# Whole 128x128 TensorE weights for the 64-query blocks of a sliding-window attention

## The chip, the cores and the metric

One core of a Trainium2 chip runs the whole program. The metric is the device time of one execution in microseconds (us), from the first to the last instruction with what the runtime puts around them. Times are medians of runs of the same program.

The engines are TensorE (PE; its weight loads are shown apart as PEld), VectorE (DVE), ScalarE (ACT), GpSimd (POOL) and SyncE (SP), which here issues all the transfers.

## The reference

Attention with a window of 128 keys and a linear bias for each head, then two MLPs. The inputs have batch 4, 8 heads, 576 positions and head dimension 64; there are 2304 tokens of width 512, and the hidden width is 2048.

```python
scores = scale * q @ k.T                         # for each batch and head, 576 x 576
rel = pos[:, None] - pos[None, :]
scores = where((rel >= 0) & (rel < 128), scores - slope[h] * abs(rel), -1e9)
attn = exp(scores - max); attn /= attn.sum(-1) + 1e-9
x = attn @ v                                     # to (2304, 512)
g = piecewise(x @ w_in1); x = g @ w_out1         # h | 0 | (h+1)^2/4
g = h2 * clip(h2 + 3, 0, 6) / 6; out = g @ w_out2    # h2 = x @ w_in2
```

## The kernel before

The queries are cut into twelve units (three for each batch of 576: 256+256+64, 192+256+128, 256+128+192, 192+256+128). A unit is computed for all eight heads, and for each head in blocks of 128 queries; a last block holds 64 queries where the unit's length is no multiple of 128. Those are unit 2 (a single block of 64), unit 3 (128 and 64), unit 8 (128 and 64) and unit 9 (128 and 64), so there are 4 x 8 = 32 blocks of 64. Units 0 to 3 are "whole": their attention is computed in plain float32, with unnormalized probabilities, and the row sum comes from a column of ones beside the values. Units 4 to 11 are "split": queries, keys, values and probabilities are split into a high and a low part of a faster format (fp32r), and the probabilities are normalized on GpSimd before they are transposed.

A step (head, block) passes through four stages, some ticks apart. `stage_a` (line 383 on) multiplies queries (the weights) with keys (moving) into PSUM on TensorE (line 380), VectorE adds the bias and finds the row's maximum (line 401), ScalarE takes the exponential (line 405), and for split units VectorE and GpSimd normalize (lines 408 to 410). Two ticks later `stage_b` transposes the probabilities on TensorE (lines 432 and 433), and ScalarE and VectorE copy and split them (lines 150 and 445). Then `stage_c_whole` (three ticks after stage a, line 463) or `stage_c` (four ticks, line 518) multiplies with the values; for whole units VectorE divides by the sums (lines 480 to 483), and `stage_d_whole` transposes the result (line 494). `prep` makes the high and low parts for a split head (lines 356 to 360, and 154/157 for the values of a pair of heads).

For a block of 64 queries the code before uses only the rows and columns that hold something: the scores' weights are 128 rows x 64 columns, the transposes have 64 rows, the value matmuls of whole units have weights of 128x64 (previous chunk of keys) and 64x64 (own chunk), and those of split units 64 rows x 128 columns for the own chunk.

Between the attention's ticks the first MLP runs in blocks of tokens: 24 matmuls per hidden chunk (12 at line 601 into `h`, 12 at line 643 into `acc`), with activations on VectorE, ScalarE and GpSimd. While the first three blocks run, its weights are also converted from float64 bits (lines 191 to 202). A hook spreads the attention's ticks over the MLP's chunks. On every engine but SP a planner orders the instructions by its own cost estimates and priorities; the order on SP is that of the program. All q, k and v transfers are on SP: for a pair of heads of a split unit keys and queries of the two heads (line 306, four transfers), then the values (lines 314 and 318). A transfer waits on SP until its buffer is free, and everything behind it on SP waits too. Keys and queries of split units have two buffers, values three.

Of the kernel before, what the change touches and what calls it, by code (L numbers as in the profile page):

```python
# [38 lines left out]
def tile_window_attention_two_mlps(  # L39
# [220 lines left out]
    class Attention:  # L260
# [19 lines left out]
        def load_whole(self, n):  # L280


            u = heads[n]
            q = self.qw[u.h // 2]
            for j in range(2):
                heads[n + j].k, heads[n + j].q = k, _ = self.kw[u.h + j], q
                nc.sync.dma_start(out=k[j * D:(j + 1) * D, :u.nk], in_=kT[u.b, u.h + j, :, u.k0:u.q1])
                if j == 0:
                    nc.sync.dma_start(out=q[:, :u.nq], in_=qT[u.b, u.h:u.h + 2, :, u.q0:u.q1].rearrange("h d n -> (h d) n"))

        def load(self, n):

            u = heads[n]
            if u.h % 2 == 0 and u.whole:
                self.load_whole(n)
            elif u.h % 2 == 0:
                self.k_owners.append(n)
                krs = self.raw.tile([P, 2, KMAX], F32, tag="kr", name=f"kr{n}")
                qrs = self.raw.tile([P, 2, UMAX], F32, tag="qr", name=f"qr{n}")
                for j in range(2):  # L300
                    heads[n + j].kr, heads[n + j].qr = krs[:, j], qrs[:, j]
                for j in range(2):
                    for dst, src, a, m in ((krs, kT, u.k0, u.nk), (qrs, qT, u.q0, u.nq)):
# [4 lines left out]
            if u.h % 2 == 0:  # L308
                self.v_owners.append(n)
                u.vt = self.vts[n // 2 % 3]  # L310
                u.vr = u.vt[:, :, 1:2 * D + 1]
                full, rest = divmod(u.nk, P)
                cols = slice(u.h * D, (u.h + 2) * D)
                nc.sync.dma_start(
                    out=u.vr[:, :full, :],
                    in_=v[u.b, u.k0:u.k0 + full * P, cols].rearrange("(c p) d -> p c d", p=P))
                if rest:
                    nc.sync.dma_start(out=u.vr[:rest, full, :],
                                      in_=v[u.b, u.k0 + full * P:u.k0 + u.nk, cols])
            else:  # L320
                u.vt, u.vr = heads[n - 1].vt, heads[n - 1].vr
# [23 lines left out]
        def prep(self, n):  # L345
# [14 lines left out]
            engines[LO["q"]].tensor_tensor(out=u.qs[:, :m], in0=u.qr[:, :m], in1=u.qs[:, :m].bitcast(F32), op=ALU.add)  # L360
            if u.h % 2 == 0:

                u.vs = self.proc.tile([P, 2, KCH, 2, D], F32R, tag="vs", name=f"vs{n}")
                full, rest = divmod(nk, P)
                parts = [(slice(0, P), slice(0, full))]
                if rest:
                    parts.append((slice(0, rest), slice(full, full + 1)))
                for pp, cc in parts:
                    for j in range(2):
                        src = u.vr[pp, cc, j * D:(j + 1) * D]  # L370
                        hi, lo = u.vs[pp, j, cc, j, :], u.vs[pp, j, cc, 1 - j, :]
                        split_hi(HI["v"], hi, src)
                        split_lo(LO["v"], lo, src, hi)
            else:
                u.vs = heads[n - 1].vs

        def scores(self, u, ps, qo, ko, m, nk):
            parts = [(u.q, u.k)] if u.whole else [(u.qs, u.kh), (u.qs, u.kl)]
            for w, (q, k) in enumerate(parts):
                nc.tensor.matmul(ps[:m, :nk], q[:, qo:qo + m], k[:, ko:ko + nk],  # L380
                                 start=(w == 0), stop=(w == len(parts) - 1))

        def stage_a(self, n, i):
# [11 lines left out]
            if u.unit == 0:  # L395
                keep_busy(ps, 2 * P)
            self.scores(u, ps, qo, ko, m, nk)
# [4 lines left out]
                out=pt[:m, :nk], in0=ps[:m, :nk], in1=dist[:m, u.h if u.whole else plain, bo:bo + nk],  # L402
                scale=-scale if u.whole else -slopes[u.h],
                scalar=3.0e38, op0=ALU.add, op1=ALU.min, accum_out=sm[:m, 0:1])
            nc.scalar.activation(out=pt[:m, :nk], in_=pt[:m, :nk], func=AF.Exp, bias=sm[:m, 0:1],  # L405
                                 scale=-1.0, accum_out=None if u.whole else sm[:m, 1:2])
            if not u.whole:
                nc.vector.tensor_scalar(out=sm[:m, 2:3], in0=sm[:m, 1:2], scalar1=EPS, scalar2=None, op0=ALU.add)  # L408
                nc.vector.reciprocal(sm[:m, 3:4], sm[:m, 2:3])  # L409
                nc.gpsimd.tensor_scalar(out=pt[:m, :nk], in0=pt[:m, :nk], scalar1=sm[:m, 3:4], scalar2=1.0,  # L410
                                        op0=ALU.mult, op1=ALU.mult)
            u.p[i] = pt

        def stage_b(self, n, i):
# [15 lines left out]
            po = P if has_prev else 0  # L430
# [3 lines left out]
            if has_prev and m == P:  # L434
                regs = [(slice(0, P), slice(0, 2), slice(s0, s0 + 2))]
            elif has_prev:
                regs = [(slice(0, P), slice(0, 1), slice(s0, s0 + 1)),
                        (slice(0, m), slice(1, 2), slice(s0 + 1, s0 + 2))]
            else:
                regs = [(slice(0, m), slice(1, 2), slice(s0 + 1, s0 + 2))]  # L440
            for pp, cs, cd in regs:
                src, hi = ps[pp, cs, :m], u.th[pp, cd, :m]
                split_hi(HI["th"], hi, src)
                if not u.whole:
                    nc.vector.tensor_tensor(out=u.tl[pp, cd, :m], in0=src, in1=hi.bitcast(F32), op=ALU.subtract)  # L445

        def stage_c_whole(self, n, i):
# [8 lines left out]
            rows = u.qbs[i][1]  # L456
            slot = 2 * i - 1 + sh
            work = [(i + sh, rows, slot + 1)]
            if slot >= 0:
                work.insert(0, (i - 1 + sh, P, slot))  # L460
            a = (2 * i + j) * (D + 1)
            for w, (c, keys, sl) in enumerate(work):
# [10 lines left out]
            nfull = u.nq // P  # L473
            parts = [(slice(0, P), slice(0, nfull))] if nfull else []
            if u.nq % P:
                parts.append((slice(0, u.nq % P), slice(nfull, nfull + 1)))
            for pp, bb in parts:
                nb = bb.stop - bb.start
                np_ = pp.stop
                nc.vector.tensor_scalar(out=rec[pp, bb], in0=r[pp, bb, 0:2 * D + 2:2 * D + 1], scalar1=EPS,  # L480
                                        scalar2=None, op0=ALU.add)
                nc.vector.reciprocal(rec[pp, bb], rec[pp, bb])
                nc.vector.tensor_tensor(
                    out=y[pp, bb], in0=r[pp, bb, 1:2 * D + 1].rearrange("p b (h d) -> p b h d", h=2),
                    in1=rec[pp, bb].rearrange("p b (h o) -> p b h o", o=1).to_broadcast([np_, nb, 2, D]), op=ALU.mult)
            u.y = y

        def stage_d_whole(self, n, i):
            u = heads[n]
            if u.h % 2 == 0 or i < len(u.qbs) - 1:  # L490
                return
            ps = psum.tile([P, BANK], F32, tag="t", name=f"x{n}")
            for b, (a, rows) in enumerate(u.qbs):
                nc.tensor.transpose(ps[:, b * P:b * P + rows], u.y[:rows, b].rearrange("p h d -> p (h d)"),
                                    ident[:rows, :rows])
            self.to_x(u, ps, LO["x_whole"])

        def stage_c(self, n, i):
# [11 lines left out]
            if i == 0 and u.prev:  # L510
                work.append((0, P, 0, u.qbs[0][1], 0))
            if i > 0:
                work.append((i - 1 + sh, P, (i - 1) * P, P + u.qbs[i][1], 2 * (i - 1) + sh))
            if last:
                work.append((i + sh, u.qbs[i][1], i * P, u.qbs[i][1], 2 * i + sh))
            for w, (c, rows, qo, nq, slot) in enumerate(work):
# [748 lines left out]
```

## Time and profile before

| what | value |
|---|---|
| median of 3 runs | 985.83 us (984.9 to 985.94) |
| the profiled execution's own time | 985.26 us |
| its span, first to last instruction | 983.5 us |
| mean granted TensorE clock | 0.998 of 2.4 GHz |
| busy: PE, PEld, DVE, ACT, POOL | 98%, 90%, 70%, 55%, 22% |
| attention's part of the span | about 4 to 515 us, beside the first MLP |

Matmuls are pipelined and their ends are modelled, so PE's busy share says little. How long TensorE takes for a matmul is read from the chain of waits, where consecutive pieces do not overlap, or from the starts of consecutive matmuls.

### The profile page before, as it was taken

The numbers are of one execution on the slowest core, as the hardware profiler recorded it, in microseconds if no ns is written. First come the engines' busy times: TensorE is split into PE (matmuls) and PEld (weight loads), VectorE is DVE, ScalarE is ACT, GpSimd is POOL, SyncE is SP. The second block draws the span as 40 slices with busy tenths as digits, with TensorE's granted clock in tenths as the row PEclk, the third lists the DMA queues.
The fourth block names the chain that finished last, engine by engine and source line by source line (L and its number), as shares of the span: only waits on it lengthen the run. The fifth ranks groups of instructions, "written<-read, shape, count | busy, mean of one in ns | idle before, by whom it ended". The sixth has DMA issues, their size and how long they took to land.

```text
span 983.5 us, 17188 instructions
## 1 busy us (share of the span) xinstructions
PE 959.4 (98%) x5771; PEld 885.4 (90%) x5771; DVE 685.6 (70%) x1768; ACT 544.3 (55%) x1334; POOL 220.7 (22%) x365
## 2 busy tenths in 40 slices
PE   8899999999999999999999999999999999999998
PEld 6787889999999998999999999999998888888987
DVE  6877886687777666767764898947747676644444
ACT  6886855577667566656653868534433334432323
POOL 2011234455455555545530000000000000000000
PEclk9999999999999999999999999999999999999999
DMA  9757313122213121222103875003354655353441
GB/s 261 218 160 240 107 52 110 51 81 82 71 43 86 50 73 42 70 70 68 52 1 118 271 274 183 1 0 118 139 182 150 207 179 161 122 156 117 117 117 68
DMA packets 95336, 114.90 MB, mean 117 GB/s; under 512 B 8848, under 2 KB 73616, under 8 KB 95248
## 3 DMA queue, kind: packets, MB, share of 16 engines
q1 hardware_dynamic: 95248, 113.80, 36.5%
q8 instruction: 46, 0.75, 0.3%
q14 instruction: 42, 0.34, 0.1%
HBM read 88.60 MB, written 25.17 MB: 116 GB/s over the span
## 4 chain that ended last, share of the span: by engine, by line
PE 80%; DVE 10%; ACT 4%; DMA 3%; issue 2%; SPq 0%; POOL 0%; ACTq 0%; DVEq 0%; POOLq 0%
PE h L601 24%; PE acc L702 17%; PE acc L643 17%; PE y L1166 5%; PE x L1166 4%; PE s L380 4%; PE r L518 3%; PE r L463 2%; PE t L432 2%; PE t L433 1%; DMA rawa<-w_out 1%; DVE kl L358 1%; DVE r L630 1%; DMA vr<-v 1%; DVE u L1175 1%
## 5 line engine op out<-in xcount | busy, mean ns | idle before, releaser
L601 PE MATMUL h<-x,wa 128*128 128x384 f32 (+1 forms) x1344 | 232.6, 318 | 4.4 <-DVE r L632 2.5
L643 PE MATMUL acc<-g,wa 128*128 128x384 f32 (+1 forms) x1344 | 229.2, 316 | 2.4 <-ACT o L150 1.2
L702 PE MATMUL acc<-wb,g 128*128 128x512 f32 x861 | 222.3, 394 | 0.0
L601 PEld LDWEIGHTS h<-x,wa 128*128 128x128 f32 x1344 | 207.6, 190 | 9.9 <-DVE r L632 3.7
L643 PEld LDWEIGHTS acc<-g,wa 128*128 128x128 f32 x1344 | 206.8, 190 | 5.7 <-ACT o L150 1.4
L702 PEld LDWEIGHTS acc<-wb,g 128*128 128x128 f32 x861 | 159.5, 188 | 24.9
L150 ACT CAST g<-r 128x384 fp32r<-128x384 f32 (+1 forms) x208 | 101.0, 487 | 81.1 <-DVE r L1113 42.6
L157 POOL TENSOR_TENSOR g<-r,g 128x256 fp32r<-128x256 f32 (+1 forms) x96 | 94.4, 985 | 196.6 <-ACT g L150 145.1
L631 ACT ACTIVATE r<-r 128x384 f32<-128x384 f32 (+1 forms) x112 | 53.3, 478 | 91.7 <-DVE r L630 90.4
L157 DVE TENSOR_TENSOR g<-r,g 128x384 fp32r<-128x384 f32 x112 | 62.3, 556 | 44.9 <-ACT g L150 44.4
L405 ACT ACTIVATE p<-p,sm 128x256 f32<-128x256 f32 (+2 forms) x160 | 75.9, 476 | 20.5 <-DVE sm L401 19.8
L630 DVE TENSOR_SCALAR r<-h 128x384 f32<-128x384 f32 (+1 forms) x112 | 55.3, 495 | 38.9 <-PE h L601 32.3
L632 DVE TENSOR_TENSOR r<-h,r 128x384 f32<-128x384 f32 (+1 forms) x112 | 55.4, 496 | 29.1 <-ACT r L631 28.5
L601 PE MATMUL h<-x,wb 128*128 128x384 f32 x384 | 72.5, 337 | 0.0
L601 PEld LDWEIGHTS h<-x,wb 128*128 128x128 f32 x384 | 68.2, 188 | 2.6
L401 DVE CUSTOM_DVE_ANT_0 p<-s,dist 128x256 f32<-128x256 f32 (+2 forms) x160 | 59.7, 374 | 14.9 <-PE s L380 13.3
L410 POOL TENSOR_SCALAR p<-p,sm 128x256 f32<-128x256 f32 (+1 forms) x104 | 47.8, 459 | 63.1 <-DVE sm L409 49.3
L360 POOL TENSOR_TENSOR qs<-qr,qs 128x256 fp32r<-128x256 f32 (+2 forms) x64 | 42.6, 665 | 26.9 <-ACT qs L357 24.4
L1112 ACT ACTIVATE r<-u 128x384 f32<-128x384 f32 x32 | 16.8, 525 | 55.6 <-DVE u L1175 55.6
L150 ACT CAST th<-t 128x256 fp32r<-128x256 f32 (+3 forms) x120 | 37.4, 312 | 14.7 <-PE t L433 12.8
L445 DVE TENSOR_TENSOR tl<-t,th 128x256 fp32r<-128x256 f32 (+3 forms) x120 | 41.6, 347 | 5.3 <-ACT th L150 4.0
L433 PE MATMUL t<-ident,p 128*128 128x128 f32 (+1 forms) x160 | 42.0, 264 | 2.7 <-DVE sm L408 2.1
(148 smaller groups left out, 1552.2 us busy)
## 6 DMA issues: line engine op xcount, KB each, us to landing
w<-wd SPq DMA_DIRECT2D x88, 256.0 KB, 2.7
rawa<-w_in SPq DMA_DIRECT2D x16, 512.0 KB, 5.5
rawa<-w_out SPq DMA_DIRECT2D x16, 512.0 KB, 5.5
rawb<-w_in SPq DMA_DIRECT2D x16, 512.0 KB, 4.2
rawb<-w_out SPq DMA_DIRECT2D x16, 512.0 KB, 5.5
wd<-sum SPq DMA_DIRECT2D x32, 256.0 KB, 2.1
wd<-wb SPq DMA_DIRECT2D x24, 256.0 KB, 2.9
out<-o SPq DMA_DIRECT2D x17, 256.0 KB, 2.2
```

The source lines that it names most:

```text
L150: nc.scalar.copy(hi, x)
L157: engines[eng].tensor_tensor(out=lo, in0=x, in1=hi.bitcast(F32), op=ALU.subtract)
L401: nc.vector.tensor_tensor_reduce(out=pt[:m, :nk], in0=ps[:m, :nk], in1=dist[:m, u.h if u.whole else plain, bo:bo + nk], scale=-scale if u. ...
L405: nc.scalar.activation(out=pt[:m, :nk], in_=pt[:m, :nk], func=AF.Exp, bias=sm[:m, 0:1], scale=-1.0, accum_out=None if u.whole else sm[:m, ...
L433: nc.tensor.transpose(ps[:m, 1, :m], pt[:m, po:po + m], ident[:m, :m])
L601: nc.tensor.matmul(ps[:, :n], self.W.w_in(a, c, f), self.x_chunk(x, b, c, n), start=(k == 0), stop=(k == 3 * KC - 1))
L630: nc.vector.tensor_scalar(out=r[:, :n], in0=ps[:, :n], scalar1=-1.0, scalar2=1.0, op0=ALU.max, op1=ALU.min)
L631: nc.scalar.activation(out=r[:, :n], in_=r[:, :n], func=AF.Square, bias=0.5, scale=0.5)
L632: nc.vector.tensor_tensor(out=r[:, :n], in0=ps[:, :n], in1=r[:, :n], op=ALU.max)
L643: nc.tensor.matmul(acc[i][:, o * n:(o + 1) * n], self.W.w_out(a, f)[:, e * P:(e + 1) * P], g[:, b, :n], start=(first and k == 0 and o == 0 ...
L702: nc.tensor.matmul(acc[t][:, :DM], g[:, b, tg * P:(tg + 1) * P], self.W.w_out(a, f), start=(first and k == 0), stop=(last and k == 2))
L1166: nc.tensor.matmul(ps[:, :N2], w[:, a, c * P:(c + 1) * P], self.x.operand(k, c, b), start=(start and n == 0), stop=(n == 5), skip_group_ch ...
```

## The change

Every block of 64 queries now uses weights of 128 rows and 128 columns. The scores read 128 query columns (64 of them zeros for split units, filled by a new GpSimd memset in `prep`, or whatever lies there for whole units). The bias, maximum and exponential run on 128 rows instead of 64. A new GpSimd memset sets the missing keys' probabilities (64 columns) to zero, the transposes are 128x128, and the value matmuls take all 128 keys. Where two instructions handled the full and the partial chunk apart (the copies of the transposes, the division by the sums, the values' high and low parts), one instruction remains.

Besides, for pairs of heads of split units the values' transfer is now issued ahead of the four transfers of keys and queries (`load_values`); for whole units it stays behind them.

```diff
         def load(self, n):
             u = heads[n]
             if u.h % 2 == 0 and u.whole:
                 self.load_whole(n)
+                self.load_values(n)
             elif u.h % 2 == 0:
+                self.load_values(n)
                 self.k_owners.append(n)
...
             engines[LO["q"]].tensor_tensor(out=u.qs[:, :m], in0=u.qr[:, :m], in1=u.qs[:, :m].bitcast(F32), op=ALU.add)
+            if m % P:
+                nc.gpsimd.memset(u.qs[:, m:m + P - m % P].bitcast(F32), 0.0)
...
-                parts = [(slice(0, P), slice(0, full))]
-                if rest:
-                    parts.append((slice(0, rest), slice(full, full + 1)))
-                for pp, cc in parts:
-                    for j in range(2):
-                        src = u.vr[pp, cc, j * D:(j + 1) * D]
...
+                for j in range(2):
+                    src = u.vr[:, :nc_, j * D:(j + 1) * D]
...
-                nc.tensor.matmul(ps[:m, :nk], q[:, qo:qo + m], k[:, ko:ko + nk],
+                nc.tensor.matmul(ps[:, :nk], q[:, qo:qo + P], k[:, ko:ko + nk],
...
+            if m < P:
+                nc.gpsimd.memset(pt[:, nk:2 * P], 0.0)
...
-                nc.tensor.transpose(ps[:, 0, :m], pt[:m, :P], ident[:m, :m])
-            nc.tensor.transpose(ps[:m, 1, :m], pt[:m, po:po + m], ident[:m, :m])
...
+                nc.tensor.transpose(ps[:, 0, :], pt[:, :P], ident)
+            nc.tensor.transpose(ps[:, 1, :], pt[:, P:] if has_prev else pt[:, :P], ident)
+            c = 0 if has_prev else 1
+            cols = P if u.whole else m
+            src, hi = ps[:, c:2, :cols], u.th[:, s0 + c:s0 + 2, :cols]
...
-                nc.tensor.matmul(u.r[:rows, a:a + D + 1], u.th[:keys, sl, :rows],
-                                 u.vt[:keys, c, j * (D + 1):(j + 1) * (D + 1)],
+                nc.tensor.matmul(u.r[:, a:a + D + 1], u.th[:, sl, :],
+                                 u.vt[:, c, j * (D + 1):(j + 1) * (D + 1)],
...
-                nc.tensor.transpose(ps[:, b * P:b * P + rows], u.y[:rows, b].rearrange("p h d -> p (h d)"),
-                                    ident[:rows, :rows])
+                nc.tensor.transpose(ps[:, b * P:(b + 1) * P], u.y[:, b].rearrange("p h d -> p (h d)"), ident)
...
-                        u.vs[:rows, j, c, :, :].rearrange("p a d -> p (a d)"),
-                        part.rearrange("p s q -> p (s q)")[:rows, slot * P:slot * P + nq],
+                        u.vs[:, j, c, :, :].rearrange("p a d -> p (a d)"),
+                        part.rearrange("p s q -> p (s q)")[:, slot * P:slot * P + nq],
```

## Rows read from the trace of the kernel before

**Rows 1.** The page's chain that ended last, shares of the span by engine.

```profile
PE 80%; DVE 10%; ACT 4%; DMA 3%; issue 2%; SPq 0%; POOL 0%; ACTq 0%; DVEq 0%; POOLq 0%
```

**Rows 2.** Stretches: length, then PE, PEld, DVE, ACT, POOL busy (xinstructions), PEclk, DMA, GB/s.

```profile
20.00:60.00 40.00, 35.52 (x244) 30.16 (x244) 35.26 (x85) 35.81 (x69) 3.10 (x3) 1.00 0.67 202
60.00:127.50 67.50, 67.18 (x473) 54.80 (x473) 52.69 (x139) 50.77 (x125) 17.66 (x16) 1.00 0.51 167
127.50:150.00 22.50, 19.55 (x132) 16.96 (x132) 20.17 (x46) 12.27 (x32) 6.66 (x8) 0.92 0.27 79
320.00:434.00 114.00, 109.18 (x679) 103.36 (x679) 78.90 (x309) 70.81 (x238) 59.56 (x110) 1.00 0.21 61
```

**Rows 3.** Groups by line and shape, PE, 60 to 127.5 us: the MLP's matmuls.

```profile
L601 PE MATMUL h<-x,wa 128*128 128x256 f32 x144 | 24.3, 300 | 0.0
L643 PE MATMUL acc<-g,wa 128*128 128x256 f32 x145 | 23.2, 295 | 0.0
```

**Rows 4.** Chain of waits, 57 to 60 us: full blocks of whole units (start, length, what).

```profile
57.55 0.43 PE s L380 x2
...
59.25 0.39 PE r L463 x4
59.64 0.12 PE t L432
```

**Rows 5.** Chain of waits, 109 to 124 us: blocks of 64 of whole units.

```profile
109.85 0.52 PE r L463 x4
110.36 0.26 PE t L433
...
119.50 0.20 PE t L432
119.71 0.06 PE t L433
119.76 0.66 PE acc L643 x4
...
120.54 0.47 PE s L380 x2
121.01 1.51 PE h L601 x11
122.52 1.44 PE acc L643 x12
```

**Rows 6.** Chain of waits at 324 us: eight attention matmuls of full split blocks.

```profile
324.11 0.39 PE r L518 x4
...
324.99 2.09 PE h L601 x12
```

**Rows 7.** PE in order of time at 363 us: eight attention matmuls of 64-blocks.

```profile
362.94 0.25 PE L518 MATMUL r<-th,vs 128*128 128x192 f32 x1
...
363.97 2.27 PE L643 MATMUL acc<-g,wa 128*128 128x384 f32 x12
```

**Rows 8.** Chain of waits at 127.5 us.

```profile
127.54 4.73 DMA vr<-v
```

**Rows 9.** PE in order of time after it.

```profile
135.78 0.39 PE L643 MATMUL acc<-g,wa 128*128 128x256 f32 x1 [1.24 <-ACT o L150]
```

**Rows 10.** SP's transfers in order of time, 110 to 126 us (start, issue).

```profile
110.39 0.38 SPq L314 DMA_DIRECT2D vr<-v  x1
...
125.67 0.53 SPq L306 DMA_DIRECT2D qr<-qT  x1
```

**Rows 11.** ACT in order of time: the first keys of a split unit.

```profile
117.78 0.54 ACT L356 ACTIVATE kh<-kr 128x384 fp32r<-128x384 f32 x1
```

**Rows 12.** The longest GpSimd group (page), and GpSimd's groups by shape: a memset.

```profile
L157 POOL TENSOR_TENSOR g<-r,g 128x256 fp32r<-128x256 f32 (+1 forms) x96 | 94.4, 985 | 196.6 <-ACT g L150 145.1
masks.py:197 POOL MEMSET ident<- 128x128 f32 x1 | 0.2, 204 | 0.0
```

**Rows 13.** Weight loads of the whole units' value matmuls: min/median/max ns, then forms.

```profile
L463 PEld LDWEIGHTS r<-vr,th x192: 128/189/228, 8.3 to 147.7; 128*128 128x128 f32 x128, 128*64 128x64 f32 x32, 64*64 64x64 f32 x32
```

More of the change, by code (lines that the diff above doesn't have):

```diff
@@ L285, in load_whole @@
             for j in range(2):
-                heads[n + j].k, heads[n + j].q = k, _ = self.kw[u.h + j], q
+                k = self.kw[u.h + j]
+                heads[n + j].k, heads[n + j].q = k, q
                 nc.sync.dma_start(out=k[j * D:(j + 1) * D, :u.nk], in_=kT[u.b, u.h + j, :, u.k0:u.q1])
@@ L289, in load_whole, with load_values @@
                     nc.sync.dma_start(out=q[:, :u.nq], in_=qT[u.b, u.h:u.h + 2, :, u.q0:u.q1].rearrange("h d n -> (h d) n"))
+        def load_values(self, n):
+            u = heads[n]
+            self.v_owners.append(n)
+            u.vt = self.vts[n // 2 % 3]
+            u.vr = u.vt[:, :, 1:2 * D + 1]
+            full, rest = divmod(u.nk, P)
+            cols = slice(u.h * D, (u.h + 2) * D)
+            nc.sync.dma_start(
+                out=u.vr[:, :full, :],
+                in_=v[u.b, u.k0:u.k0 + full * P, cols].rearrange("(c p) d -> p c d", p=P))
+            if rest:
+                nc.sync.dma_start(out=u.vr[:rest, full, :],
+                                  in_=v[u.b, u.k0 + full * P:u.k0 + u.nk, cols])
         def load(self, n):
@@ L360, in prep, with scores @@
             engines[LO["q"]].tensor_tensor(out=u.qs[:, :m], in0=u.qr[:, :m], in1=u.qs[:, :m].bitcast(F32), op=ALU.add)
+            if m % P:
+                nc.gpsimd.memset(u.qs[:, m:m + P - m % P].bitcast(F32), 0.0)
             if u.h % 2 == 0:
                 u.vs = self.proc.tile([P, 2, KCH, 2, D], F32R, tag="vs", name=f"vs{n}")
-                full, rest = divmod(nk, P)
-                parts = [(slice(0, P), slice(0, full))]
-                if rest:
-                    parts.append((slice(0, rest), slice(full, full + 1)))
-                for pp, cc in parts:
-                    for j in range(2):
-                        src = u.vr[pp, cc, j * D:(j + 1) * D]
-                        hi, lo = u.vs[pp, j, cc, j, :], u.vs[pp, j, cc, 1 - j, :]
-                        split_hi(HI["v"], hi, src)
-                        split_lo(LO["v"], lo, src, hi)
+                nc_ = -(-nk // P)
+                for j in range(2):
+                    src = u.vr[:, :nc_, j * D:(j + 1) * D]
+                    hi, lo = u.vs[:, j, :nc_, j, :], u.vs[:, j, :nc_, 1 - j, :]
+                    split_hi(HI["v"], hi, src)
+                    split_lo(LO["v"], lo, src, hi)
             else:
                 u.vs = heads[n - 1].vs
-        def scores(self, u, ps, qo, ko, m, nk):
+        def scores(self, u, ps, qo, ko, nk):
             parts = [(u.q, u.k)] if u.whole else [(u.qs, u.kh), (u.qs, u.kl)]
             for w, (q, k) in enumerate(parts):
-                nc.tensor.matmul(ps[:m, :nk], q[:, qo:qo + m], k[:, ko:ko + nk],
+                nc.tensor.matmul(ps[:, :nk], q[:, qo:qo + P], k[:, ko:ko + nk],
                                  start=(w == 0), stop=(w == len(parts) - 1))
@@ L396, in stage_a @@
                 keep_busy(ps, 2 * P)
-            self.scores(u, ps, qo, ko, m, nk)
+            self.scores(u, ps, qo, ko, nk)
             pt = self.work.tile([P, 2 * P], F32, tag="p", name=f"p{n}_{i}", bufs=LAG_B + 1)
@@ L401, in stage_a @@
             nc.vector.tensor_tensor_reduce(
-                out=pt[:m, :nk], in0=ps[:m, :nk], in1=dist[:m, u.h if u.whole else plain, bo:bo + nk],
+                out=pt[:, :nk], in0=ps[:, :nk], in1=dist[:, u.h if u.whole else plain, bo:bo + nk],
                 scale=-scale if u.whole else -slopes[u.h],
-                scalar=3.0e38, op0=ALU.add, op1=ALU.min, accum_out=sm[:m, 0:1])
-            nc.scalar.activation(out=pt[:m, :nk], in_=pt[:m, :nk], func=AF.Exp, bias=sm[:m, 0:1],
-                                 scale=-1.0, accum_out=None if u.whole else sm[:m, 1:2])
+                scalar=3.0e38, op0=ALU.add, op1=ALU.min, accum_out=sm[:, 0:1])
+            nc.scalar.activation(out=pt[:, :nk], in_=pt[:, :nk], func=AF.Exp, bias=sm[:, 0:1],
+                                 scale=-1.0, accum_out=None if u.whole else sm[:, 1:2])
+            if m < P:
+                nc.gpsimd.memset(pt[:, nk:2 * P], 0.0)
             if not u.whole:
-                nc.vector.tensor_scalar(out=sm[:m, 2:3], in0=sm[:m, 1:2], scalar1=EPS, scalar2=None, op0=ALU.add)
-                nc.vector.reciprocal(sm[:m, 3:4], sm[:m, 2:3])
-                nc.gpsimd.tensor_scalar(out=pt[:m, :nk], in0=pt[:m, :nk], scalar1=sm[:m, 3:4], scalar2=1.0,
+                nc.vector.tensor_scalar(out=sm[:, 2:3], in0=sm[:, 1:2], scalar1=EPS, scalar2=None, op0=ALU.add)
+                nc.vector.reciprocal(sm[:, 3:4], sm[:, 2:3])
+                nc.gpsimd.tensor_scalar(out=pt[:, :nk], in0=pt[:, :nk], scalar1=sm[:, 3:4], scalar2=1.0,
                                         op0=ALU.mult, op1=ALU.mult)
@@ L429, in stage_b @@
             s0 = 2 * i if u.prev else 2 * i - 1
-            po = P if has_prev else 0
+            assert has_prev or m == P
             if has_prev:
-                nc.tensor.transpose(ps[:, 0, :m], pt[:m, :P], ident[:m, :m])
-            nc.tensor.transpose(ps[:m, 1, :m], pt[:m, po:po + m], ident[:m, :m])
[L434 to L445, printed above, removed]
+                nc.tensor.transpose(ps[:, 0, :], pt[:, :P], ident)
[3 more added lines that the diff above has]
+            src, hi = ps[:, c:2, :cols], u.th[:, s0 + c:s0 + 2, :cols]
+            split_hi(HI["th"], hi, src)
+            if not u.whole:
+                nc.vector.tensor_tensor(out=u.tl[:, s0 + c:s0 + 2, :cols], in0=src, in1=hi.bitcast(F32), op=ALU.subtract)
         def stage_c_whole(self, n, i):
@@ L455, in stage_c_whole @@
             sh = 1 if u.prev else 0
-            rows = u.qbs[i][1]
             slot = 2 * i - 1 + sh
-            work = [(i + sh, rows, slot + 1)]
+            work = [(i + sh, slot + 1)]
             if slot >= 0:
-                work.insert(0, (i - 1 + sh, P, slot))
+                work.insert(0, (i - 1 + sh, slot))
             a = (2 * i + j) * (D + 1)
-            for w, (c, keys, sl) in enumerate(work):
-                nc.tensor.matmul(u.r[:rows, a:a + D + 1], u.th[:keys, sl, :rows],
-                                 u.vt[:keys, c, j * (D + 1):(j + 1) * (D + 1)],
+            for w, (c, sl) in enumerate(work):
+                nc.tensor.matmul(u.r[:, a:a + D + 1], u.th[:, sl, :],
+                                 u.vt[:, c, j * (D + 1):(j + 1) * (D + 1)],
                                  start=(i == 0 and j == 0 and w == 0), stop=(w == len(work) - 1),
@@ L472, in stage_c_whole @@
             r = u.r[:, :QB * 2 * (D + 1)].rearrange("p (b c) -> p b c", b=QB)
[L473 to L485, printed above, removed]
+            nb = len(u.qbs)
+            rec, r, y = rec[:, :nb], r[:, :nb], y[:, :nb]
+            nc.vector.tensor_scalar(out=rec, in0=r[:, :, 0:2 * D + 2:2 * D + 1], scalar1=EPS, scalar2=None, op0=ALU.add)
+            nc.vector.reciprocal(rec, rec)
+            nc.vector.tensor_tensor(
+                out=y, in0=r[:, :, 1:2 * D + 1].rearrange("p b (h d) -> p b h d", h=2),
+                in1=rec.rearrange("p b (h o) -> p b h o", o=1).to_broadcast([P, nb, 2, D]), op=ALU.mult)
             u.y = y
@@ L492, in stage_d_whole @@
             ps = psum.tile([P, BANK], F32, tag="t", name=f"x{n}")
-            for b, (a, rows) in enumerate(u.qbs):
-                nc.tensor.transpose(ps[:, b * P:b * P + rows], u.y[:rows, b].rearrange("p h d -> p (h d)"),
-                                    ident[:rows, :rows])
+            for b in range(len(u.qbs)):
+                nc.tensor.transpose(ps[:, b * P:(b + 1) * P], u.y[:, b].rearrange("p h d -> p (h d)"), ident)
             self.to_x(u, ps, LO["x_whole"])
@@ L510, in stage_c @@
             if i == 0 and u.prev:
-                work.append((0, P, 0, u.qbs[0][1], 0))
+                work.append((0, 0, u.qbs[0][1], 0))
             if i > 0:
-                work.append((i - 1 + sh, P, (i - 1) * P, P + u.qbs[i][1], 2 * (i - 1) + sh))
+                work.append((i - 1 + sh, (i - 1) * P, P + u.qbs[i][1], 2 * (i - 1) + sh))
             if last:
-                work.append((i + sh, u.qbs[i][1], i * P, u.qbs[i][1], 2 * i + sh))
-            for w, (c, rows, qo, nq, slot) in enumerate(work):
+                work.append((i + sh, i * P, u.qbs[i][1], 2 * i + sh))
+            for w, (c, qo, nq, slot) in enumerate(work):
                 for part in (u.th, u.tl):
```

11 lines of the change are left out of this document (removed).

## The prediction

> **What bounds the kernel now.** I read the chain of waits first: it lies on TensorE for 80% of the span [rows 1], so the question is how TensorE spends its time in the stretches that hold 64-query blocks. The code says where they are: units 2 and 3 are scored from about 60 us to 135 us, units 8 and 9 from about 320 us to 434 us. The table of stretches then says how much room the other engines have [rows 2]. In 60 to 127.5 us VectorE is busy 52.69 of 67.5 us (78%), ScalarE 75%, GpSimd 26%; in 127.5 to 150 us VectorE is at 90%. In 320 to 434 us VectorE is at 69%. TensorE stands still for hardly anything in the first of these, so a faster TensorE makes that stretch shorter until VectorE stops it.
>
> Last I priced narrow against whole matmuls. The busy times can't be used for that (modelled ends), so I took pieces of the chain, which tile the time. A full MLP matmul with 256 moving columns takes 1.44/12 = 0.12 us [rows 5]. In 60 to 127.5 us there are 144 + 145 = 289 of these [rows 3], together 34.7 us. The other 473 - 289 = 184 matmuls [rows 2] got the remaining 32.8 us, 0.178 us each, while whole attention matmuls take about 0.11: four value matmuls 0.39, a transpose 0.12 [rows 4]. Something in the narrow ones costs more than it saves.
>
> **The change on TensorE, whole units (2 and 3).** Per block of 64, from single groups:
> - Scores, two matmuls with 64-column weights: 0.47 for the pair, and the eleven MLP matmuls behind it take 1.51 instead of 11 x 0.12 = 1.32, so 0.66 [rows 5]. With 128 columns and 256 moving the pair is 0.43 [rows 4]; two matmuls cannot be under 2 x 0.11 = 0.22; at 192 moving columns I take the middle, 0.33. Saved 0.33.
> - Transposes: 0.20 + 0.06, and the four MLP matmuls behind them take 0.66 instead of 0.48: 0.44 [rows 5]. Whole: 2 x 0.12 = 0.24 [rows 4]. Saved 0.20.
> - Values: four narrow matmuls 0.52 and the whole transpose behind them 0.26 [rows 5], against 0.39 + 0.12 [rows 4]. Saved 0.27.
>
> That is 0.80 x 16 blocks = 12.8 us, if each group stood alone. Where narrow groups adjoin, the extra time at entry and exit is paid once. The budget of the stretch includes that: 184 matmuls at 0.11 are 20.2 us, the 15 score pairs in it cost 15 x (0.33 - 0.22) = 1.6 us more, together 21.8; they took 32.8, so 11.0 us are excess. The remainder after 127.5 us (a score pair, two groups of transposes, two of values: 0.33 + 0.40 + 0.54) adds 1.3. I take 12.3 us as what TensorE can save.
>
> **On TensorE, split units (8 and 9).** A tick with a 64-block has eight attention matmuls between MLP groups and takes 363.97 - 362.94 = 1.03 us [rows 7]; eight matmuls of full blocks take 324.99 - 324.11 = 0.88 us [rows 6]. Those are no narrower in moving columns on the whole, so 0.15 each: 16 x 0.15 = 2.4 us. Part of it could vanish in TensorE's waits for VectorE there (it is idle for some 5 us of the 114 [rows 2]); against that, the merged split of the values takes instructions out of the same VectorE work. I let the two cancel: 2.4, bounds 0 and 4.
>
> **The values asked for earlier.** One values transfer is on the chain: issued at 127.54, landed 4.73 us later [rows 8], behind four transfers of keys and queries, the first of which had held SP until 125.67 [rows 10]. ScalarE waits for it in `prep`, the weights' conversion is queued behind that on ScalarE, VectorE waits for the conversion, and TensorE stands idle for 1.24 us at 135.78 [rows 9]. The granted clock of the stretch is 0.92 [rows 2]: 22.5 x 0.08 / 0.5 = 3.6 us of it at 1.2 GHz, right after that pause, which costs 1.8. Issued ahead of the keys, the transfer no longer sits behind SP's wait and is first of its five, so ScalarE need not wait. Worth 0 (VectorE at 90% would stop TensorE there anyway) to 3.0 us.
>
> What is moved past: keys and queries of a split pair now stand behind a values transfer that may wait for its buffer. In steady state a values buffer (three) comes free before a keys buffer (two), so nothing. At the change from whole to split units it does wait: the first one goes out at 110.39 [rows 10], when the whole unit's value matmuls have let go of the buffer, and the keys of the same pair, until now ahead of it, follow by 113 us. They land between 116 and 118 us (3 us, or the 4.7 of rows 8) and are read at 117.78 [rows 11]. A loss of at most a few tenths on ScalarE; I count nothing, and both move with TensorE.
>
> **Added and merged elsewhere.** 32 memsets of 128x64 on the probabilities and 16 on the queries, on GpSimd. A memset of 128x128 took 0.204 us [rows 12]; between 0.1 and 0.2 us each, up to 10 us on an engine that is busy 24 of 90 us in the first stage and 60 of 114 in the second. They hide in GpSimd's idle time, since the transposes come two ticks later; cover gone, see the rivals. Instructions on 128 rows instead of 64 cost the same, by their columns. The merged copies, divisions and splits lower VectorE, ScalarE and GpSimd a little (twelve VectorE instructions in unit 3's divisions); I count nothing.
>
> **What the first stage really gives.** TensorE alone: 12.3 + 3.0 = 15.3 us off 60 to 150 us. But VectorE has 52.69 + 20.17 = 72.9 us of work in these 90 us. The densest stretches show 88% (20 to 60 us, where TensorE also has pauses) to 90% [rows 2]; at 88% the stage needs 82.8 us, which gives 7.2; at 92%, beyond what is shown, 79.2 us and 10.8. Twelve fewer VectorE instructions help by another 1 to 2 us. I take 11.0, between 7.2 and 15.3.
>
> **Sum.** 985.26 (the profiled execution's own time) - 11.0 - 2.4 = 971.9. This execution is 0.57 us under the median of the runs, so 972.4 there.
>
> **Rivals.**
> 1. VectorE stops it early: 7.2 us in the first stage, nothing in the second (its savings go into waits). 985.83 - 7.2 = 978.6. For it: 90% before 150 us and a planner that orders by its own costs; against: the merges.
> 2. TensorE is free to take everything: 15.3 + 4 = 19.3, so 966.5. For it: TensorE's pauses in 60 to 127.5 us sum to next to nothing. Against: VectorE's 72.9 us would have to run at 97%.
> 3. Slower, by weight loads. A load of 64 columns took 128 ns at least, one of whole weights 189 at the median [rows 13]. If loads set TensorE's pace, 160 loads (64 for scores, 32 for own-chunk transposes, 64 for values) get 0.06 us longer each: 9.8 us, 995.6. It decides from the point where narrow matmuls are quicker than whole ones in sequence. Against: four narrow value matmuls take 0.52, four whole ones 0.39 [rows 4, 5]. The Trainium skill, "TensorE: Matmul & The Clock Gate", section LDWEIGHTS, has the load's time proportional to the number of columns (columns / 1.2 ns), which by itself would make whole weights about 53 ns dearer per load, an estimate from that page of 8.5 us in all. By that rule the trace agrees on the load's own duration, not on what the sequence takes.
> 4. Slower, by GpSimd's queue. Each of the 32 memsets sits in order behind `g` instructions of 0.985 us that often wait for ScalarE [rows 12]. If every transpose waited for one of them, 32 x 0.985 = 31.5 us would be lost and 13.4 won: 1003.9. From 0.42 us per block on it eats the gain. Against: two ticks of slack.
> 5. Nothing: the excess is not the shapes' but that of short groups among MLP matmuls, and stays. 985.8. Against: whole groups of the same lengths show none.
>
> **How the numbers follow.** The forecast (969 to 976) 0.50; rival 1 (976 to 981) 0.20; rival 2 (under 969) 0.15, of which 0.04 under 966; rival 3 0.03; rival 4 0.06; rival 5 0.06. Under 0.2% (2 us) a change of this kernel can't be told from none. Faster 0.50 + 0.20 + 0.15 = 0.85, the same 0.06, slower 0.09. The range 966 to 981 leaves out 0.04 above the faster end and 0.15 at the other, some 0.19; the forecast's own range is 969 to 976.
>
> **What would show it.** Right: a score pair of a 64-block with the MLP matmuls behind it at 0.33 instead of 0.66; whole-unit value groups at 0.39; the eight-matmul tick of units 8 and 9 at 0.88; the stretch of the first stage some 11 us shorter at VectorE 88 to 92%; no transfer of values on the chain near 125 us and the granted clock at 1.00 there. Wrong: transposes released by GpSimd's memset; ScalarE waiting for `kr`; VectorE's chain ahead of TensorE all through 60 to 140 us; or another pause with a fall of the clock elsewhere, since the planner orders anew.

## The result and the profile after

The changed kernel took 967.62 us (median of 4 runs, 966.61 to 969.24) against 985.59 us for the kernel before on the same chip: a ratio of 0.982, 95% interval 0.9803 to 0.9837. It is 18.0 us faster, where 13.4 was forecast. The profiled execution took 968.46 us with a span of 966.7, so the two profiles are 16.8 us apart. Of these, following the first MLP's matmuls one by one in both traces, 12.4 us come from the first stage (the 576th matmul starts 12.94 us earlier than before, the first 0.57 earlier already), 3.8 from units 8 and 9 (from the 1512th to the 2304th), and the rest before, between and after. Of the first stage's gain 11.3 us are there by the 400th matmul, which now starts at 118.8 us instead of 130.7; only 1.0 comes behind it. Each trace is of one execution, and those of one kernel lie up to some 2 us to either side of their median, so stage differences of about 1 us are weak.

The chain's shares by engine in the kernel after, which answer to [rows 1]:

```profile
PE 79%; DVE 10%; ACT 4%; DMA 3%; issue 2%; POOL 0%; SPq 0%; ACTq 0%; DVEq 0%; POOLq 0%
```

The shares are as they were: a chain that was TensorE's is TensorE's still, only shorter. Stretches of the kernel after (columns as in [rows 2]) show where:

```profile
60.00:137.00 77.00, 74.16 (x604) 72.33 (x604) 72.93 (x175) 63.66 (x142) 28.40 (x41) 0.99 0.54 173
60.00:115.00 55.00, 54.90 (x457) 54.12 (x457) 51.34 (x130) 49.37 (x108) 19.22 (x30) 1.00 0.62 200
115.00:137.00 22.00, 19.26 (x150) 18.21 (x150) 21.59 (x46) 14.29 (x34) 9.18 (x12) 0.97 0.35 105
135.50:139.00 3.50, 3.50 (x17) 3.50 (x18) 2.88 (x13) 1.58 (x5) 2.36 (x4) 0.51 0.78 228
371.00:374.50 3.50, 3.50 (x15) 3.50 (x14) 1.73 (x9) 1.71 (x6) 1.52 (x4) 0.51 0.60 166
```

The 473 + 132 = 605 matmuls that filled 60 to 150 us [rows 2] now fill 77 us. VectorE has the same 72.9 us of work in them, so its share rose from 81% to 95%. ScalarE is at 83%, GpSimd at 37%. The stage has two parts: up to 115 us TensorE is never idle for long (54.90 of 55 us), and in the last 22 us VectorE is at 98% while TensorE is idle for 2.7 us. The last two rows are stretches at a granted clock of 0.51, that is 1.2 GHz. Each follows a pause of TensorE (below).

The chain of the kernel after, 63.6 to 69.5 us, answers to [rows 5]: blocks of 64 between MLP matmuls.

```profile
63.64 0.12 PE t L438
63.75 0.11 PE t L439
63.86 0.33 PE s L384 x2
...
66.81 0.32 PE s L384 x2
67.13 0.82 PE acc L635 x7
...
69.03 0.39 PE r L462 x4
```

A score pair takes 0.33 us with no surcharge on what follows (seven MLP matmuls in 0.82, 0.117 each), two transposes 0.23, four value matmuls 0.39. In the second stage, TensorE in order of time:

```profile
365.13 0.25 PE L510 MATMUL r<-th,vs 128*128 128x192 f32 x1
...
365.97 0.71 PE L635 MATMUL acc<-g,wa 128*128 128x384 f32 x3
```

The eight attention matmuls of a tick start 0.84 us before the next MLP group; it was 1.03 [rows 7]. The median of all such ticks without a wait from the 1512th to the 2064th MLP matmul went from 1.02 to 0.84.

SP's transfers in order of time show the moved step: the values of the pair of heads that had to wait in [rows 8] now go out first of their five. ScalarE splits them (`vs`) without a wait; before, it waited 2.38 us for them.

```profile
115.19 0.37 SPq L300 DMA_DIRECT2D vr<-v  x1
115.61 0.53 SPq L324 DMA_DIRECT2D kr<-kT  x1
```

```profile
117.67 0.36 ACT L154 CAST vs<-vr 128x192 fp32r<-128x192 f32 x1
```

No values transfer is on the chain of 60 to 140 us any more. From 112.0 to 125.2 us it runs through VectorE and ScalarE alone, most of it pieces of the weights' conversion, while TensorE works off what it has. Two pieces of the chain there, and what is on it at the end of the stage:

```profile
112.34 0.94 DVE ma L198
...
125.23 0.50 PE s L384 x2
...
132.17 0.49 ACT qs L363
132.66 0.94 ACT wa L150
...
133.63 1.38 DVE wa L157
...
135.41 2.81 PE h L593 x12
```

ScalarE and VectorE make the parts of the next split head and a piece of converted weights, one behind the other, and TensorE stands for 0.86 and 0.73 us before 134.0 and 135.4 us. Then twelve matmuls take 2.81 us instead of 1.44 [rows 5]: that is the stretch at 0.51. The second pause lies in units 8 and 9 (chain):

```profile
368.09 1.02 DVE x L157
...
370.20 0.43 POOL p L416
...
370.68 0.33 PE t L438
...
371.42 3.58 PE h L593 x12
```

A transpose waits 1.62 us for GpSimd's normalization, which waited for VectorE. The twelve matmuls of 384 columns behind it take 3.58 us; such a group took 2.27 at full clock [rows 7].

### The profile page after: what moved, and what is told of

It is laid out like the page before. It is cut to its first block, busy times and chain, and to the rows that moved or that the text cites. A ratio compares the mean times of both kernels' runs of the same rounds, so it can differ in the third digit from the quotient of the medians.

```text
span 966.7 us, 17170 instructions
## 1 busy us (share of the span) xinstructions
PE 944.1 (98%) x5771; PEld 887.9 (92%) x5771; DVE 687.5 (71%) x1734; ACT 541.5 (56%) x1292; POOL 224.4 (23%) x397
## 4 chain that ended last, share of the span: by engine, by line
PE 79%; DVE 10%; ACT 4%; DMA 3%; issue 2%; POOL 0%; SPq 0%; ACTq 0%; DVEq 0%; POOLq 0%
PE h L593 25%; PE acc L635 17%; PE acc L694 17%; PE y L1158 5%; PE x L1158 4%; PE s L384 3%; PE r L510 2%; PE t L438 2%; PE r L462 2%; PE t L439 1%; DVE r L1105 1%; DVE sum L917 1%; DVE u L1167 1%; ACT g L150 1%; ACT r L1104 1%
## 5 line engine op out<-in xcount | busy, mean ns | idle before, releaser
L1104 ACT ACTIVATE r<-u 128x384 f32<-128x384 f32 x32 | 16.8, 525 | 55.9 <-DVE u L1167 55.9
L439 PE MATMUL t<-ident,p 128*128 128x128 f32 x160 | 43.5, 273 | 0.5 <-ACT th L150 0.5
L438 PE MATMUL t<-ident,p 128*128 128x128 f32 x128 | 37.6, 297 | 4.9 <-POOL p L416 2.5
L445 DVE TENSOR_TENSOR tl<-t,th 128x256 fp32r<-128x256 f32 (+1 forms) x104 | 39.3, 378 | 2.9 <-ACT th L150 1.9
```

The costliest lines, as they stand in the source:

```text
L438: nc.tensor.transpose(ps[:, 0, :], pt[:, :P], ident)
```

## The experiments

The variants of the first three groups start from the kernel before and take over parts of the change.

**The order of the values alone, and the shapes alone.** The first takes over only this edit; the second takes over all the others.

```diff
             elif u.h % 2 == 0:
+                self.load_values(n)
                 self.k_owners.append(n)
```

> The kernel before with nothing but the values of split units asked for ahead of their keys. Theory A (the gain is that of the shapes on TensorE): 984 to 986 us, the values transfer leaves the chain near 127 us, but little comes of it, at most 1.5 us. Theory B (the order carries what the forecast of 13.4 us lacked, some 3 to 5 us, by the pause at 135 us and the fall of the clock behind it): 981 to 982.5 us, and no stretch at half clock.

> All the wide shapes, with keys ahead of values as before. Theory A: 967 to 969 us, as the whole change. Theory B: 971 to 972.5 us, with a values transfer on the chain at the step from whole to split units.

The order alone: 985.12 us, ratio 0.9992 (0.9981 to 1.0003), nothing that can be told from no change. This is theory A's number. The shapes alone: 972.62 us, 0.9861 (0.9849 to 0.9874), beside theory B's (0.1 us above it). So neither theory holds by itself: the order is worth (0.9861 - 0.9820) x 985.6 = 4.0 us once the shapes are whole. The two do not add: 0.8 us alone, 4.0 us on top. The chain of the kernel with the shapes alone says why:

```profile
120.08 3.09 DMA vr<-v
...
123.19 0.35 ACT vs L161
...
124.38 0.95 ACT wa L157
...
125.35 1.24 DVE wa L164
...
126.61 0.59 ACT o L157
...
127.25 0.79 PE acc L673 x3
```

and its stretches right behind that:

```profile
122.00:127.50 5.50, 3.10 (x23) 2.56 (x23) 2.15 (x4) 3.83 (x11) 1.86 (x4) 1.00 0.06 20
127.50:131.00 3.50, 3.50 (x18) 3.50 (x18) 3.50 (x7) 0.73 (x4) 0.73 (x1) 0.51 0.22 75
```

It is the chain of the kernel before (values transfer, `prep` on ScalarE, conversion, VectorE, TensorE), with more lost in it: ScalarE waits 4.50 us for `vr` where it waited 2.38, TensorE is busy 3.10 of 5.5 us, and the clock falls for 3.5 us, and once more at 141 us. The transfer lands 9.1 us sooner than before (123.2 against 132.3 us), but TensorE is 10.9 us further by then (start of its 400th MLP matmul). Up to that matmul the shapes alone gain 11.3 us, as much as the whole change does; behind it they lose 3.0, where the whole change gains 1.0. So their first stage gained only 8.3 us, and the change's 12.4. What is lost there is not the shapes' price but the late transfer's.

**The shapes in whole units alone, and in split units alone** (the order of the transfers as before). A switch for each kind of unit selects the old or the new form of every edit:

```diff
-                nc.tensor.matmul(ps[:m, :nk], q[:, qo:qo + m], k[:, ko:ko + nk],
+                r = P if wide(u, "s") else m
+                nc.tensor.matmul(ps[:r, :nk], q[:, qo:qo + r], k[:, ko:ko + nk],
...
```

> Wide shapes in units 2 and 3 alone, old order of transfers. Theory A: 13 us of the 18 are theirs: 972 to 974 us, with VectorE at 92 to 95% between 60 us and the first split unit. Rival (what TensorE gives back there is taken by VectorE as the forecast had it, and the planner's order gave the rest): 975 to 978 us.

> Wide shapes in units 8 and 9 alone, old order of transfers. Theory A (a tick of eight matmuls goes from 1.03 to 0.84 us, 16 x 0.19 = 3.0 us, and one or two us less waiting behind the merged splits): 980.5 to 982.5 us. Rival (the savings go into waits for VectorE, as the forecast let part of them): 983 to 985 us.

Whole units: 975.84 us, 0.9896 (0.9883 to 0.9909); its first stage gained 8.4 us, and the second lost 0.9. That is the rival's number, but not for the rival's reason: up to the 400th matmul it gains 11.5 us, and the late values transfer is on its chain, as with the shapes alone. Split units: 980.37 us, 0.9943 (0.9931 to 0.9955), theory A's number within 0.1 us; its second stage gained 5.1 us. It has no low clock in the stretch that answers to [rows 2]:

```profile
320.00:434.00 114.00, 110.21 (x712) 108.70 (x712) 84.67 (x294) 70.50 (x220) 61.73 (x124) 1.00 0.23 67
```

So the second stage's shapes are worth 5.1 us. Of these, 3.7 are in the attention matmuls between the MLP groups (34.2 us before, 30.5 now) and 1.0 in shorter waits of TensorE (5.4 and 4.4). The changed kernel gets 3.8 of the 5.1. The transpose's wait of 1.62 us stands in both kernels; what only the changed one has is the half clock behind it.

**The scores alone, and scores with transposes,** in all units, by the same switch.

> Only the scores of the 64-query blocks get 128-column weights; transposes and value matmuls stay narrow, transfers in the old order. By the prices of the prediction a whole-unit score pair goes from 0.66 to 0.33 us (16 of them, 5.3 us), a split pair saves some 0.05 us; where a narrow group stood beside it, the entry is still paid by that group: 4 to 5 us in all, 980.5 to 982 us. Rival (the excess is not the shape's but that of short groups among MLP matmuls): the pair stays at 0.6 us and the time at 985.

> Scores and transposes of the 64-query blocks wide, value matmuls and the result's transposes narrow, transfers in the old order. Transposes add 16 x 0.2 us in the whole units and about 0.1 us each in the split ones: 3 to 4 us more than the scores alone, 977 to 978.5 us, of the 972.6 us that all wide shapes reach in the old order. Rival (GpSimd's memset delays the transposes): no gain over the scores alone and transposes released by the memset.

Scores: 983.07 us, 0.9971 (0.9958 to 0.9985). With the transposes: 977.09 us, 0.9908 (0.9888 to 0.9928). With the value matmuls too it is the kernel of the shapes alone, 972.62. So each of the three groups brings something: 2.9, 6.2 and 4.6 us, as 0.0029, 0.0063 and 0.0047 of 985.7. The scores alone missed their number (4 to 5 us expected), and the transposes brought more than theirs (3 to 4). The place counts: with the scores alone the first stage is 1.9 us shorter and the second 1.1 us longer.

In whole units the price itself came as expected. From the last MLP matmul ahead of a score pair to the second one behind it TensorE took 0.90 us before and 0.56 with whole score weights, at each of the four places where a pair stands between MLP groups. That 1.9 us came of it and not 5.3 fits the prediction's remark that adjoining narrow groups pay entry and exit once: the transposes and values beside the other pairs were still narrow.

In split units the ticks of eight say which matmuls cost. Their median is 1.02 us before, 1.10 with whole scores, 1.11 with whole transposes too, and 0.84 once the value matmuls are whole. With scores and transposes whole a tick looks like this:

```profile
356.67 0.25 PE L548 MATMUL r<-th,vs 128*128 128x192 f32 x1
...
356.96 0.29 PE L548 MATMUL r<-th,vs 64*128 64x64 f32 x1
...
357.78 2.29 PE L673 MATMUL acc<-g,wa 128*128 128x384 f32 x12
```

The two value matmuls with 64 rows keep the whole surcharge; whole score weights bring nothing in split units, and what the transposes brought there is mostly shorter waits of TensorE (5.8 and then 3.2 us).

**What a narrow matmul costs by itself.** The changed kernel gets one more matmul of 64 moving columns ahead of each of the 72 score pairs of units 4 to 7, 10 and 11, which are all of full blocks. It writes where the pair then writes, so no result changes. Its weights are whole, 64 columns wide, or 64 rows high.

```diff
+            if u.unit in (4, 5, 6, 7, 10, 11):
+                nc.tensor.matmul(ps[:128, :64], u.qs[:128, qo:qo + 128], u.kh[:128, ko:ko + 64], ...)  # whole
+                nc.tensor.matmul(ps[:64, :64], u.qs[:128, qo:qo + 64], u.kh[:128, ko:ko + 64], ...)    # 64 columns
+                nc.tensor.matmul(ps[:128, :64], u.qs[:64, qo:qo + 128], u.kh[:64, ko:ko + 64], ...)    # 64 rows
```

> The changed kernel with one more matmul ahead of each of the 72 score pairs of split units 4 to 7, 10 and 11 (128x128 weights, 64 moving columns, its result overwritten by the pair). If a whole matmul costs its place in the weight-load sequence, about 0.11 us, the 72 of them cost 8 us at most, less where TensorE waits for VectorE there: 5 to 8 us over the changed kernel.

> The same place and count, with weights of 128 rows and 64 columns. If going into and out of a narrow shape costs time (0.09 us in, 0.09 to 0.16 out, as the differences of starts in the kernel before suggest), each costs 0.2 to 0.35 us: 14 to 25 us over the changed kernel, so 6 to 17 more than the whole probe. Rival (a load takes time by its number of columns, so half the columns are quicker): no more than the whole probe, 3 to 8 us.

> The same place and count, with weights of 64 rows and 128 columns. If any change of shape has this price, rows as well as columns: 14 to 25 us over the changed kernel. If only the number of weight columns counts: as the whole probe, 5 to 8 us.

Against the kernel before: whole 0.9885 (0.987 to 0.990), 974.37 us; 64 columns 0.986 (0.9841 to 0.988), 971.27; 64 rows 1.0045 (1.0028 to 1.0061), 989.88. The whole one met its number. The 64 columns fell to the rival: no dearer than whole ones. The 64 rows met the first of their two numbers: 22 us over the changed kernel, and (1.0045 - 0.9885) x 986.25 = 15.8 us over whole weights, for 72 matmuls. From the 576th to the 1512th MLP matmul, where 43 of the 72 stand, at a granted clock of 1.00, the three took 174.2, 174.1 and 185.1 us, the changed kernel 170.7. TensorE in order of time, whole first:

```profile
257.37 0.27 PE L442 MATMUL t<-ident,p 128*128 128x128 f32 x1
257.40 0.28 PE L384 MATMUL s<-kh,qs 128*128 128x64 f32 x1
257.51 0.36 PE L387 MATMUL s<-kh,qs 128*128 128x256 f32 x1
...
257.83 1.90 PE L638 MATMUL acc<-g,wa 128*128 128x384 f32 x10
```

64 columns:

```profile
256.13 0.27 PE L442 MATMUL t<-ident,p 128*128 128x128 f32 x1
256.16 0.27 PE L384 MATMUL s<-kh,qs 128*64 128x64 f32 x1
256.27 0.37 PE L387 MATMUL s<-kh,qs 128*128 128x256 f32 x1
...
256.60 2.24 PE L638 MATMUL acc<-g,wa 128*128 128x384 f32 x12
```

64 rows:

```profile
262.25 0.27 PE L442 MATMUL t<-ident,p 128*128 128x128 f32 x1
262.45 0.29 PE L384 MATMUL s<-kh,qs 64*128 64x64 f32 x1
262.68 0.39 PE L387 MATMUL s<-kh,qs 128*128 128x256 f32 x1
...
263.02 2.27 PE L638 MATMUL acc<-g,wa 128*128 128x384 f32 x12
```

From the transpose to the MLP group: 0.46, 0.47 and 0.77 us (medians of all places: 0.46, 0.46 and 0.77); the busy times (0.28, 0.27, 0.29) show nothing of that. The time is in the starts: the 64-row matmul begins 0.20 after the transpose instead of 0.03, and the next one 0.23 after it instead of 0.11. Groups of weight loads, 150 to 300 us, of the 64-column and then of the 64-row kernel (busy, mean | idle of the loads just before), show where it waits:

```profile
L384 PEld LDWEIGHTS s<-kh,qs 128*64 128x64 f32 x42 | 5.8, 137 | 0.4
```

```profile
L384 PEld LDWEIGHTS s<-kh,qs 64*128 64x128 f32 x39 | 7.1, 183 | 7.0 <-issue 4.0 <-PE r L513 0.8 <-DVE r L625 0.3
```

The load of 64 columns is short and follows at once, and it still wins nothing, since a whole matmul's place in the sequence is 0.11 us anyway. The load of 64 rows is as long as a whole one, but the load engine stands idle 7.0 / 39 = 0.18 us before each: it is not begun under the matmuls ahead.

The Trainium skill, "TensorE: Matmul & The Clock Gate", section LDWEIGHTS, says that a load takes time by its columns and not by its rows. The durations here agree (137 ns for 64 columns, 183 for 64 rows); the time of the sequence goes the other way. The Trainium skill, "TensorEngine Tiling (Array Packing)", section Key Properties, says that a change of the tiling mode drains TensorE, with no price. Whether 64-row weights among whole ones are such a change no run shows. What the trace has is 0.31 us for rows, in and out, and nothing for columns in these units.

**Is VectorE what now holds the first stage?** Two kernels get 48 more memsets on VectorE in units 2 and 3 (7.2 us of busy time more on the page of the one without the change, 5.5 on the other), one without and one with the change; a third takes work off VectorE in the changed kernel.

```diff
+            if u.unit in (2, 3):
+                for _ in range(2):
+                    nc.vector.memset(zeros, 0.0)
...
-            split_lo("dve", hl[:, 1], m, hl[:, 0])
+            split_lo("pool" if self.nm == "a" and f >= 5 and f % 2 else "dve", hl[:, 1], m, hl[:, 0])
```

> The kernel before with two more VectorE memsets of a small tile that nobody reads, in each of the 24 steps of units 2 and 3 (48 in all, about 0.17 us each, some 8 us of VectorE). If VectorE is not the bound there (81% busy), it hides most: 985.6 + 1 to 3 us. If it was the bound already: + 6 to 8 us.

> The changed kernel with the same 48 VectorE memsets. If VectorE is what now stops TensorE there (95% busy), nearly all of the 8 us show: 967.6 + 5 to 8 us. If TensorE or the order of the values still bounds it: + 1 to 3 us, as in the kernel before.

> The changed kernel with the low parts of odd chunks from 5 on of the first MLP's first weights made on GpSimd instead of VectorE. If VectorE, busy 95% in the first stage, holds TensorE there, the stage gets shorter by what leaves VectorE: 963 to 966 us. If VectorE is only nearly full and TensorE still sets the pace, or GpSimd's longer instruction delays what the second half of the MLP reads: 967 to 972 us.

With the load the kernel before took 1008.85 us, 1.023 (1.0209 to 1.0251), some 23 us more; the changed one 984.65, 17 more. Both missed every expectation, at two to three times the work added (48 x 0.165 = 7.9 us). Their stretches, without and then with the change:

```profile
60.00:100.00 40.00, 38.34 (x213) 28.84 (x212) 24.09 (x89) 23.08 (x61) 4.44 (x4) 0.79 0.55 174
```

```profile
60.00:100.00 40.00, 33.71 (x253) 31.66 (x252) 31.35 (x104) 28.70 (x61) 7.50 (x16) 0.96 0.68 217
```

VectorE is less busy than without the load, in the same 40 us: 24.09 against 30.31 us in the kernel before, 31.35 against 36.78 in the changed one. TensorE gets through fewer matmuls there too, 213 instead of 268 and 253 instead of 330, at a granted clock of 0.79 and 0.96. The planner laid the instructions out anew; which part of that costs the time was not followed up. This pair says nothing on the question.

With low parts moved to GpSimd the time was 971.34 us, 0.9852 (0.9838 to 0.9867): 3.2 us slower than the change, the rival's number. VectorE and then GpSimd in order of time:

```profile
122.35 3.38 DVE L202 CUSTOM_DVE_ANT_0 ma<-rawa,ma 128x2048 uint16<-128x2048 uint16 x1
...
125.98 0.41 DVE L476 TENSOR_TENSOR y<-r,rec 128x256 f32<-128x256 f32 x1
...
122.29 2.35 POOL L157 TENSOR_TENSOR wa<-ma,wa 128x1024 fp32r<-128x1024 f32 x1
```

and what waited for it on TensorE:

```profile
126.54 0.66 PE L487 MATMUL x<-ident,y 128*128 128x128 f32 x2 [3.18 <-DVE y L476]
```

VectorE's conversion took 3.38 us beside GpSimd's, where 1.22 is its median, and everything behind it on VectorE came late. So VectorE's queue can stop TensorE at the end of this stage. In the changed kernel it does: VectorE is at 98% from 115 to 137 us, and the chain lies on it from 112.0 on. The most that a freer VectorE could give there is an estimate from the changed kernel's rows: the 2.7 us that TensorE is idle and the 1.4 us of the half-clock stretch (2.81 - 1.44), some 4 us. How much of it can be had is not shown, because GpSimd was not a free place for the work.

## Why the prediction was right, step by step

The time lies in the range and below the forecast's own (969 to 976), in the part that was given to rival 2. The mechanism held in TensorE's prices and in the chain behind the late values; three sizes were off, and that the sum came near is in part luck.

- **Prices of whole shapes in whole units.** Right: 0.33, 0.23 and 0.39 us against 0.33, 0.24 and 0.39. The narrow score pair's price was right too: 0.34 us more than the whole one, where 0.33 was forecast.
- **The split units' term of 2.4.** Mis-sized: 3.8 measured, 5.1 where no clock fell. The tick is 0.84, not 0.88, and 16 x (1.03 - 0.84) = 3.0. TensorE's waits swallowed nothing of it; they became 1.0 us shorter. In the runs by parts they shrank with the transposes' edits (5.8 to 3.2 us) and grew again with the values' (4.3), so the merged split of the values, on which the text counted, shows no gain. The cause given, narrow weights as such, was half of it: 64 columns cost nothing in these units, 64 rows 0.31 us.
- **The first stage's 11.0.** 12.4 measured. The step that failed is VectorE's ceiling of 88 to 92%: it ran at 95% over 77 us. VectorE did become the limit that the text expected, but only from some 112 us on: in 60 to 115 us TensorE was busy 54.90 of 55. Up to the 400th matmul TensorE gave back 11.3 us, close to the 11.0 of the budget up to 127.5 us.
- **The values, 0 to 3.0 in that sum.** The chain of cause was right, its worth misplaced. Alone it gave 0.8 us; with whole shapes 4.0, and the shapes alone gave 8.3 in this stage and not 12.3. The text let VectorE decide between the ends, but it was the faster TensorE that made the late transfer dearer. The sum came out near because the one error fills the other, and that was luck. (A slip of reading beside it: of the four transfers ahead of the values the second, the queries', waited until 125.67 us [rows 10], not the first.)
- **The clock of 1.00 near there.** Wrong in part: the fall after the values' wait is gone, and another came at 135.5 us behind other pauses, and one at 371. That was named as what could go wrong.
- **Memsets and keys at nothing.** Nearly right: 15 memsets on probabilities of 0.15 us lie between 60 and 140 us, and the only transpose that waits for GpSimd there waits for a normalization. In units 8 and 9 one transpose waited 0.5 us for a memset on probabilities, at 337 us, and VectorE waited once for one, 1.0 us; another weight load waited 0.8 us for the queries' memset. The keys' transfers are not on the chain.
- **Rivals.** 1 (VectorE early), 3 (weight loads) and 5 (nothing) fell with the result and with the runs by parts; 4 (GpSimd's queue) shows in two waits of 0.86 and 1.62 us, at 133 and 369 us, for normalizations, and in the one of 0.5 us for a memset. Rival 2 was nearest, 1.1 us below the result.

What stays open: which instruction the planner would have to move to lose the pauses at 133 and 369 us, and how much of the some 4 us at the end of the first stage a freer VectorE would give. Why 64 columns cost 0.34 us at a plain float32 score pair and nothing in split units (fp32r) is not shown either: the probes are of split units, and no run puts a single narrow matmul into whole ones.

## What to carry to other kernels

Price a narrow matmul by the starts of its neighbours, not by its duration or its load's: here 64 rows among whole weights cost 0.31 us, 64 columns in fp32r neither cost nor saved, and 64 columns at a pair of plain float32 score matmuls cost 0.34. Where one engine gets faster, look again at each transfer that was hidden before: an edit that is worth nothing alone (0.8 us) may be worth 4.0 after the other. Adding or moving work to test for a bound is no clean test under a planner: 48 small instructions, 7.9 us of work, cost 17 to 23 us.

## What the runs showed of the hardware

- Half-clock stretches of some 3.5 us (granted 0.51) came behind pauses of TensorE in most variants and at other places in each (127.5 and 141 us with the shapes alone, 135.5 and 371 with the whole change). A pause alone does not tell: the same transpose's wait of 1.62 us was followed by half clock in the changed kernel (371 us) and not in the one with the split units' shapes alone (1.00 throughout). With only the values moved there was none in these stages, though it has the slower shapes; but its profiled execution was the fastest of twelve (982.25 us, median 985.12).
- A VectorE instruction that took 1.21 to 1.65 us in the changed kernel took 3.38 while a 2.35 us GpSimd instruction started just ahead of it. It was no single case: with the low parts on GpSimd, six such GpSimd instructions ran before 140 us, and each of the five VectorE conversion steps that began under one (lines 198, 200 and 202) ended 0.5 to 1.1 us behind its end, whenever it had begun. Shorter VectorE instructions under them (lines 405, 476, 622 and 624) took no longer than elsewhere.
